# Both transposes of the global probabilities and the next pair's scores in one stop between the products

## The chip, the cores and the metric

The kernel runs on one core of a Trainium2 chip. The metric is the device time of one execution in microseconds (us), as the median of several executions; lower is better. TensorE (PE in the profile) does matrix products and transposes into PSUM banks, ScalarE (ACT), VectorE (DVE) and GpSimd (POOL) do the element-wise work, SyncE (SP) issues the transfers between HBM and SBUF. [...]

## The reference, cut to what matters

Eight batches, eight heads of size 64, 512 local and 32 global tokens. Attention comes first; its output, as rows of 512 channels over 32 + 512 tokens, goes through a feed-forward block ("channel mix") with a hidden width of 1024.

```python
# attention: a local token sees all 32 global keys and the local keys within 32 places
s_g = scale * q_g @ concat(k_g, k_l).T;  out_g = softmax(s_g) @ concat(v_g, v_l)
s_l = concat(scale * q_l @ k_g.T, where(|i - j| <= 32, scale * q_l @ k_l.T, -1e9))
out_l = softmax(s_l) @ concat(v_g, v_l)
x = concat(out_g, out_l) as (8, 544, 512)
# channel mix
xk = mu_k * x + (1 - mu_k) * x_prev;  xr = mu_r * x + (1 - mu_r) * x_prev
k  = relu(xk @ w_k) ** 2
out = sigmoid(xr @ w_r) * (k @ w_v)
```

Everything is float32. The large products of the channel mix are each made of three reduced-precision products of high and low parts (high by high, high by low, low by high), so every operand exists as a pair: xkh and xkl, xrh and xrl, bh and bl, wk_h and wk_l.

## The kernel before, in words

**The work in a step.** While the channel mix of one batch runs, the attention of the next batch is made in its gaps. `batch_of_heads()` yields attention in four-head halves ("pairs" of units, two pairs to a batch), and the channel mix is a generator that yields after each product of 24 matmuls of 128x256, about 2.7 us of TensorE. A string in the table BATCH (L1352) says in which order the two take turns: F is one product, A is one *stop*, the piece of attention that stands between two products. The order in which the code emits TensorE's instructions is the order in which TensorE runs them, since `in_line` (L149) chains each to the one before.

**The stops of a pair.** `attention()` (L917) yields these stops for a pair:
- T: transposes of the local probabilities Pt (L439, shown as ps_t or ps_s <- ident,Pt), copied to SBUF by ACT at L448;
- U0: `transposes_global(Pg, 0)`, three transposes of the global probabilities Pg into one PSUM bank, which two ACT copies (L532 and L538) take to the tensor PT;
- U1: `transposes_global(Pg, 1)`, three more, with one ACT copy (L532), and behind them in the same stop S, the scores of the next pair (ps_s <- raw_qk);
- GW: the next pair's global scores G, and W, the products of probabilities and values (ps_s <- PT,raw_v), after which the next raw_v are loaded.

The last pair of all has no next pair and so neither S nor G.

**Banks.** From the second batch on `psum(tag)` hands out banks by MIDDLE_USE (L132): "m" (products) has three, "s" (scores, W, some transposes) four, and "t" (transposes) has **one**. What takes bank t waits until the copy has read what was there before.

**What ACT, DVE and POOL do in between.** After the score stop the softmax pieces wait in the queue `softmaxes`; `soften()` emits one at each F. For each keys product ACT does relu (L694) and square (L695, to a block B). From the third batch on (FROM = 2) the second product of the block, k by w_v, uses seven products in place of eight, on sums and differences of blocks (B11, B12, ..., T1 to T4). `Keys.difference` makes such a T on DVE (L772); `Keys.part` makes its high part on ACT (L779, bh) and its low part bl (L780): on DVE where the block's name begins with B, on POOL where it begins with T. The other operand of these products, a, is loaded from scratch by SP (L338).

**The end.** `end()` runs the last products alone, with no attention in between; a table of steps gives what is prepared after each product, and `at("T3", 1)` stands first in it.

Of the kernel before, what the change touches and what calls it, by code (L numbers as in the profile page):

```python
# [10 lines left out]
F32 = mybir.dt.float32  # L11
# [9 lines left out]
P = 128  # L21
# [14 lines left out]
def window_of(i):  # L36
    return min(max(i - 1, 0), NW - 1)
# [28 lines left out]
FIRST = """  # L66
    @qk0 @qk1 B.1 B.0 G.a+5 g.a @qk3 S.a1 @qk2 F.a @ch5 R.a1.0 S.a0 E.a1.0 R.a1.1 @ch4 J.a R.a0.0 A.5 G.b
    R.a0.1 E.a1.1 S.b0 E.a0.1 g.b M.a I.a1 A.4 N.a1.1 f.S.b1+4 U.a.1 @ch2 @v0 D.5 U.a.0 @v1 E.a0.0 u.a.1 S.b1 I.a0 N.a1.0
    T.a1.0+2 u.a.0 D.4 N.a0.1 N.a0.0 @ch1 T.a1.1 C.a1.0 C.a1.1 F.b T.a0.1 T.a0.0 C.a0.1 A.2 R.b0.0 D.2 C.a0.0
    R.b0.1 @ch6 J.b A.1 E.b0.0 H.5 R.b1.0 D.1 H.2 @ch3 A.6 L.5 @qkc1 f.G.c+3 P.a0 p.a0 H.4 f.G.c+4 P.a1 E.b0.1 R.b1.1 I.b0 L.2  # L70
    @qkc0 p.a1 @ch0 @ch7 M.b X.0.k.0 N.b0.0 G.c T.b0.0 E.b1.1 Y.0.k.0 X.0.r.0 D.6 g.c C.b0.0 Z.0.k.0 E.b1.0 A.0
    A.3 U.b.1 u.b.1 N.b0.1 T.b0.1 A.7 D.3 C.b0.1 U.b.0 I.b1 u.b.0 D.7 Y.0.r.0 Z.0.r.0 S.c1 R.c1.0 H.6 L.4 @v2
    D.0 @v3 P.b0 H.1 H.7 @ch10 N.b1.0 p.b0 S.c0 N.b1.1 @qkd0 L.6 X.0.k.2 H.3 E.c1.0 T.b1.0 L.1 A.10 L.3 T.b1.1
    Y.0.k.2 H.0 R.c1.1 @ch11 C.b1.1 L.7 D.10 A.11 C.b1.0 X.0.r.2 L.0 E.c1.1 Z.0.k.2 R.c0.0 @ch9 @qkd1 D.11 I.c1
    H.10 F.c P.b1 L.10 K.0.0 p.b1 Y.0.r.2 H.11 R.c0.1 k.0.0 E.c0.1 A.9 N.c1.1 L.11 G.d T.c1.1 N.c1.0 Z.0.r.2 D.9
# [15 lines left out]
def local_global_attention_then_rwkv_ffn(  # L91
# [10 lines left out]
    nc = tc.nc  # L102
    B = qk.shape[0]
# [37 lines left out]
    def psum(tag):  # L141
        n = turn[tag] = turn.get(tag, -1) + 1
        pool = use[tag][n % len(use[tag])]
        return pool.tile([P, 512], F32, tag="ps", name=f"ps_{tag}")
# [17 lines left out]
    def transpose(*a, **kw):  # L162
        return in_line(nc.tensor.transpose(*a, **kw))  # L163
# [12 lines left out]
    for r in range(len(ROWS[0])):  # L176
        rows, same = slice(r * CK, (r + 1) * CK), {}
        for g, row in enumerate(ROWS):
            at = START[window_of(row[r])] // CK
# [3 lines left out]
        for (n, off), gs in same.items():  # L183
# [5 lines left out]
            part = edge[rows, (off + 1) // 2, rows]  # L189
# [93 lines left out]
    FROM = 2  # L283
# [65 lines left out]
    def load_qk(s, pool=rawp, tag=""):  # L349
        s.qk = pool.tile([P, K0 + SK + 2 * NC], F32, tag="qk" + tag, name="raw_qk")  # L350
        nc.sync.dma_start(out=s.qk, in_=qk[s.b, s.c])
        s.q, s.k, s.mu = s.qk[:, QG:K0], s.qk[:, K0:K0 + SK], s.qk[:, K0 + SK:]

    def load_v(s, pool=rawp, tag=""):
        raw = pool.tile([P, NV], F32, tag="v" + tag, name="raw_v")
        nc.sync.dma_start(out=raw, in_=v[s.b, s.c])
        s.v = raw.rearrange("p (h w d) -> p h w d", h=2, d=D)
# [68 lines left out]
    def scores(slots):  # L426
        r = Scores(slots)
        r.make()
        r.read(0)
        r.read(1)  # L430
        return r

    def whole(s):
        return [(s, p) for p in range(2)]
# [24 lines left out]
    class Global:  # L459
# [4 lines left out]
        whole = None  # L464
# [53 lines left out]
    def tails(rows, at, step, n):  # L518
        first = PT[rows, 0, 0, at:at + CK]
        return bass.AP(first.tensor, first.offset, (first.ap[0], (PART, 4), (step, n), (1, CK)))  # L520

    def transposes_global(Pg, part, n_fill=0):
        ts = ((0, 1, 5), (2, 3, 4))[part]
        tp = psum("t")[:, :3 * P].rearrange("p (t n) -> p t n", n=P)
        fill(tp[:, 0], n_fill)
        for n, t in enumerate(ts):
            lo, hi = (t * (W - CK), (t + 1) * (W - CK)) if t < 5 else (NGK - W, NGK)
            transpose(tp[:hi - lo, n], Pg[:, lo:hi], ident)

        def copy():  # L530
            n, rows = (2 if 5 in ts else 3), slice(0, W - CK)
            nc.scalar.copy(  # L532
                tails(rows, TAIL[ts[0]], TAIL[ts[1]] - TAIL[ts[0]], n),
                tp[rows, 0:n].rearrange("p t (u q) -> p u t q", u=4),
            )
            if 5 in ts:
                rows = slice(P - 2 * CK, P)
                nc.scalar.copy(tails(rows, TAIL[5], CK, 1), tp[rows, 2:3].rearrange("p t (u q) -> p u t q", u=4))  # L538
        return copy
# [73 lines left out]
    class Tokens:  # L613
# [19 lines left out]
        def part(self, x):  # L633
            return (self.xk_h, self.xk_l) if x == "k" else (self.xr_h, self.xr_l)
# [105 lines left out]
    class Keys:  # L740
# [30 lines left out]
                self.k[out] = self.k[place] if place else self.block(out)  # L771
            nc.vector.tensor_sub(self.k[out][i], self.k[a][i], self.k[b][i])  # L772

        def part(self, b, i):
            tags = Keys.PARTS[Keys.n_parts % len(Keys.PARTS)]
            Keys.n_parts += 1
            h, l = (self.tokens[0].two(mlp, f"b{x}", F32R, tag) for x, tag in zip("hl", tags))
            val = self.k[b][i]
            nc.scalar.copy(h, val)  # L779
            (nc.vector if b[0] == "B" else nc.gpsimd).tensor_sub(l, val, h.bitcast(F32))  # L780
            self.parts.setdefault(b, []).append((h, l))

        def made(self, b, i):
# [133 lines left out]
    def attention(pairs, R, Pg):  # L917

        for pair, nxt in zip(pairs, pairs[1:] + [None]):
            for s in nxt or ():  # L920
                load_qk(s)
            halves_of = [iter(range(2)) for _ in R]
            for j, r in enumerate(R):
                whole_unit = pair[0].b > FROM + 1
                for copies in [["t", "s"]] if whole_unit else [["t"], ["t"]]:
                    done = [transposes(r, next(halves_of[j]), j, bank=bank) for bank in copies]
                    for copy in done:
                        copy()
                    yield
            transposes_global(Pg, 0)()  # L930
            yield
            transposes_global(Pg, 1)()
            if nxt:
                R = [scores(whole(s)) for s in nxt]
                halves = list(product(R, range(2)))
                halves[0][0].exps(0)
                for (r, h), (r_next, h_next) in zip(halves, halves[1:]):
                    softmaxes.append((lambda r=r, h=h: r.norm(h), lambda r=r_next, h=h_next: r.exps(h)))
            yield
            if nxt:  # L940
                G = Global(nxt)
                G.make("s", "t")
                G.read()
                Pg = G.Pg
            weighted(pair, True)()
            if nxt:
                softmaxes.append((lambda: R[1].norm(1), G.exps))
                softmaxes.append((G.norm,))
            for s in nxt or ():
                load_v(s)  # L950
            yield pair[1].c + 1 == NC
# [47 lines left out]
    group_g = {y: Global(pair) for y, pair in pair_of.items()}  # L999
    first = tokens_of(0)  # L1000
    mus = {"k": mu_k_sb, "r": mu_r_sb}
    copies, banks, got = {}, {}, {}
# [4 lines left out]
    def fill(bank, n):  # L1007
        while n > 0:
            k = min(n, 4)
            blocks = bass.AP(ident.tensor, ident.offset, (ident.ap[0], (0, k), (1, P)))  # L1010
            matmul(bank[:, :k * P].rearrange("p (t n) -> p t n", t=k), ident, blocks, start=True, stop=True)
            n -= k
# [19 lines left out]
        group_g[y].make(*("tt" if y in "ab" else "st"), n_fill, (lambda: group["a1"].ahead(1)) if y == "a" else None)  # L1032

    def step_transposes_global(y, part, n_fill=0):
        copies["U", y, part] = transposes_global(group_g[y].Pg, int(part), n_fill)

    def step_weighted(x, n_fill=0):
        if len(x) > 1:
# [166 lines left out]
    with tc.manual_schedule(engines={mybir.EngineType.SP}):  # L1205
        for x in FIRST:
            x, _, n_fill = x.partition("+")
            kind, at = (x[0], x[1:]) if x[0] == "@" else (x[0], x[2:])
# [136 lines left out]
    def keys_at(b):  # L1345
# [4 lines left out]
    ends, held_writes = [], []  # L1350
    FILL_AT = {(B - 2, 1): (1, 0)}
    BATCH = {  # L1352
        FROM - 1: "AFAFAFAFAF" "AFFAFFF" "AFAFAFAFAF" "AFFAFFF",
        FROM: "AFAFAFAFAF" "AFAF" "AFAFAFAFAF" "AFFAFF",
        None: "AFFAFFAF" "AFFAFF" "AFFAFFAF" "AFFFAFF",
    }
    last = first[1]
    change_use(MIDDLE_USE)
    for b in range(1, B):
        if b < B - 1:  # L1360
# [4 lines left out]
            last = keys_at(b) if b >= FROM else batch.last  # L1365
    t, = final.tokens
# [3 lines left out]
    last = keys_of[B - 1]  # L1370

    def end():
        keys, gates = final.keys(t), t.gates()
        values, outs = chain(ends[0], last.values_2()), final.values_of_one()
        at = last.part
        todo = (
            lambda: (at("T3", 1), at("T1", 0), last.difference("T4", 1)),
            lambda: (at("T1", 1), at("T4", 0), held_writes.pop()()),
            lambda: t.mixing("r0"),
            lambda: (at("T4", 1), at("B22", 0)),  # L1380
            lambda: t.mixing("r2"),
            lambda: at("B22", 1),
            lambda: final.part("B11", 0),
            lambda: (final.part("B11", 1), final.part("B21", 0)),
            lambda: final.part("B21", 1),
        )
        for n, x in enumerate("VKVKVKVKVEGEGEE"):
            next({"K": keys, "V": values, "E": outs, "G": gates}[x], None)
            if n < len(todo):
                todo[n]()  # L1390
            yield
    for _ in end():
        pass
# [49 lines left out]
```

## Time and profile before

| | |
|---|---|
| median of 3 runs | 631.14 us (630.88 to 631.23) |
| the profiled execution | 631.95 us, of which the profile's span is 630.2 us |
| TensorE busy | 621.4 us, 99% of the span |
| DVE, ACT, POOL busy | 437.8 (69%), 381.8 (61%), 335.2 us (53%) |
| granted TensorE clock | tenths of full speed: 9 (90% or more) in all 40 slices |
| chain of waits | 82% TensorE, then DVE 5%, DMA 3%, POOL 3% |

The profile is one execution as the hardware profiler recorded it. In a row of the timeline the first number is the start in us from the beginning of the span, the second the time from the start of the first to the end of the last of the instructions that the row takes together. Matmuls overlap, so their pace is read from the distance between starts, not from the length of one.

### The profile page before, as it was taken

The page shows a single profiled execution, that of the slowest core. Times are in us where ns is not written, and L with a number is a line of the kernel's source. Part 1 is how long each engine was busy: PE and PEld are TensorE (multiplying, and loading weights), DVE is VectorE, ACT ScalarE, POOL GpSimd, SP SyncE. Part 2 cuts the span into 40 slices and gives each one's busy share as a digit, 9 for nine tenths or more (in the row PEclk, how much of TensorE's full clock was granted, in tenths as well). Part 3 has the DMA queues.
Part 4 walks back from the last instruction along what each step waited for, and adds up shares of the span by engine and source line. Part 5 has one row for each costly group of instructions (what it writes and reads, how often), then busy time and mean ns, then how long its engine had stood idle before and what let it go on. Part 6 is the DMA issues. An engine that isn't in the chain of part 4 may idle for free.

```text
span 630.2 us, 20466 instructions
## 1 busy us (share of the span) xinstructions
PE 621.4 (99%) x8354; PEld 592.7 (94%) x8354; DVE 437.8 (69%) x1238; ACT 381.8 (61%) x1154; POOL 335.2 (53%) x292
## 2 busy tenths in 40 slices
PE   7999999999999999999999999999999999999997
PEld 4789999999999999999999999999999999999997
DVE  8999983659888487666686677667686647446750
ACT  6999967264373778575747757575757744433531
POOL 4786555536855335845375535745375535533740
PEclk9999999999999999999999999999999999999999
DMA  8965561457393546275563928275553734467673
GB/s 335 407 206 207 206 230 63 167 206 263 105 304 128 200 164 228 66 272 210 173 245 122 355 92 340 83 266 201 190 228 118 286 102 136 129 222 238 202 244 138
DMA packets 43278, 127.29 MB, mean 202 GB/s; under 512 B 3760, under 2 KB 20656, under 8 KB 43184
## 3 DMA queue, kind: packets, MB, share of 16 engines
q1 hardware_dynamic: 43184, 125.98, 56.1%
q8 instruction: 66, 1.08, 0.6%
q14 instruction: 28, 0.23, 0.1%
HBM read 108.66 MB, written 17.30 MB: 200 GB/s over the span
## 4 chain that ended last, share of the span: by engine, by line
PE 82%; DVE 5%; DMA 3%; POOL 3%; issue 1%; ACT 1%; SPq 0%; DVEq 0%; POOLq 0%
PE ps_m L160 64%; PE ps_s L160 12%; PE ps_t L163 3%; DMA w<-w_v 1%; PE ps_s L163 1%; DMA raw_qk<-qk 1%; DMA raw_v<-v 1%; DVE a L299 1%; POOL wk_l L271 1%; DVE diff L656 1%; POOL Pt L420 1%; POOL w L252 1%; PE ps_t L160 1%; DVE diff L651 0%; POOL wv_l L271 0%
## 5 line engine op out<-in xcount | busy, mean ns | idle before, releaser
L160 PE MATMUL ps_m<-xkh,wk_h 128*128 128x256 f32 x544 | 154.5, 284 | 0.0
L160 PE MATMUL ps_m<-xkh,wk_l 128*128 128x256 f32 x544 | 151.0, 278 | 0.0
L160 PE MATMUL ps_m<-xkl,wk_h 128*128 128x256 f32 x544 | 150.9, 277 | 0.0
L160 PE MATMUL ps_m<-bh,a 128*128 128x256 f32 x736 | 132.5, 279 | 0.0
L160 PEld LDWEIGHTS ps_m<-bh,a 128*128 128x128 f32 x736 | 113.5, 188 | 0.0
L420 POOL TENSOR_TENSOR Pt<-Pt,ssum 128x512 f32<-128x512 f32 x64 | 69.4, 1089 | 81.7 <-ACT Pt L409 38.4
L409 ACT ACTIVATE Pt<-Pt,m 128x128 f32<-128x128 f32 x256 | 99.5, 397 | 11.9 <-DVE m L402 11.8
L160 PEld LDWEIGHTS ps_m<-xkh,wk_h 128*128 128x128 f32 x544 | 102.4, 188 | 3.7 <-issue 1.2
L160 PEld LDWEIGHTS ps_m<-xkh,wk_l 128*128 128x128 f32 x544 | 102.3, 188 | 0.0
L160 PEld LDWEIGHTS ps_m<-xkl,wk_h 128*128 128x128 f32 x544 | 102.3, 188 | 0.0
L160 PE MATMUL ps_m<-bl,a 128*128 128x256 f32 x368 | 102.1, 277 | 0.0
L694 ACT ACTIVATE relu<-ps_m 128x512 f32<-128x512 f32 x52 | 31.0, 596 | 76.6 <-PE ps_m L160 76.6
L160 PE MATMUL ps_m<-xrh,wr_h 128*128 128x256 f32 x272 | 76.8, 282 | 0.0
L661 POOL TENSOR_TENSOR xkl<-xfull,xkh 128x512 fp32r<-128x512 f32 x30 | 40.2, 1340 | 66.1 <-DVE ssum L361 42.8
L160 PE MATMUL ps_m<-xrl,wr_h 128*128 128x256 f32 x272 | 75.3, 277 | 0.0
L160 PE MATMUL ps_m<-xrh,wr_l 128*128 128x256 f32 x272 | 75.3, 277 | 0.0
L402 DVE CUSTOM_DVE_ANT_0 Pt<-ps_s,masks 128x128 f32<-128x128 f32 x256 | 55.8, 284 | 22.3 <-PE ps_s L160 22.3
L160 PEld LDWEIGHTS ps_m<-bl,a 128*128 128x128 f32 x368 | 69.2, 188 | 0.0
L661 POOL TENSOR_TENSOR xrl<-diff,xrh 128x512 fp32r<-128x512 f32 x30 | 41.1, 1368 | 41.3 <-DVE xrh L660 26.1
L780 DVE TENSOR_TENSOR bl<-B,bh 128x512 fp32r<-128x512 f32 x40 | 37.8, 960 | 30.0 <-ACT bh L779 29.7
L780 POOL TENSOR_TENSOR bl<-B,bh 128x512 fp32r<-128x512 f32 x36 | 49.0, 1382 | 17.5 <-ACT bh L779 11.7
L656 DVE SCALAR_TENSOR_TENSOR diff<-diff,mu_r_sb,xT 128x256 f32<-128x256 f32 x56 | 57.0, 1057 | 0.0
(158 smaller groups left out, 1474.4 us busy)
## 6 DMA issues: line engine op xcount, KB each, us to landing
a<-scratch SPq DMA_DIRECT2D x92, 512.0 KB, 4.7
raw_v<-v SPq DMA_DIRECT2D x32, 896.0 KB, 8.4
raw_qk<-qk SPq DMA_DIRECT2D x32, 628.0 KB, 4.9
out_l<-gate SPq DMA_DIRECT2D x32, 256.0 KB, 2.2
w<-w_k SPq DMA_DIRECT2D x8, 512.0 KB, 11.9
w<-w_v SPq DMA_DIRECT2D x8, 512.0 KB, 3.6
w<-w_r SPq DMA_DIRECT2D x4, 512.0 KB, 3.8
scratch<-wv_h SPq DMA_DIRECT2D x8, 256.0 KB, 2.3
```

Of the source, the lines that this page charges most:

```text
L160: return in_line(nc.tensor.matmul(*a, **kw))
L163: return in_line(nc.tensor.transpose(*a, **kw))
L252: nc.gpsimd.tensor_scalar(word(n, F32, 1), word(n, F32, 1), REBIAS, 1.0, op0=ALU.mult, op1=ALU.mult)
L271: nc.gpsimd.tensor_sub(part_of_weights(n, "l"), word(n, F32, 0), part_of_weights(n, "h").bitcast(F32))
L299: nc.vector.tensor_sub(s.bitcast(F32R), s, hs.bitcast(F32))
L402: nc.vector.tensor_tensor_reduce(out=self.Pt[:, i], in0=self.place(t, n, h), in1=masks[:, 2 * self.slots[t][1] + n], op0=ALU.add, op1=ALU. ...
L409: nc.scalar.activation(self.Pt[:, i], self.Pt[:, i], AF.Exp, bias=self.low_x[:, i:i + 1], scale=-1.0, accum_out=self.ssum[:, i:i + 1],)
L420: nc.gpsimd.tensor_mul(self.Pt[:, some], self.Pt[:, some], inv.unsqueeze(2).to_broadcast([P, 4, W]))
L656: nc.vector.scalar_tensor_tensor(self.shape(xf[:, j]), self.shape(d[:, j]), mu[:, c0 + j:c0 + j + 1], self.prev(c0 + j), op0=ALU.mult, op1 ...
L661: nc.gpsimd.tensor_sub(lo[:, both], xf, hi[:, both].bitcast(F32))
L694: nc.scalar.activation(rk, kp, AF.Relu)
L780: (nc.vector if b[0] == "B" else nc.gpsimd).tensor_sub(l, val, h.bitcast(F32))
```

## The change

`transposes_global` gets the bank as a parameter. `attention()` no longer yields between U0 and U1, and puts the scores between them: the stop is now U0, S, U1. U0 stays in bank t, except for the last pair, where it takes a bank of "s". A pair has one stop fewer, so the strings in BATCH lose one A per pair; the number of F's stays the same. With batch 3 and later, a first pair had T FF T FF U0 F (U1 S) FF (GW) FF and now has T FF T FF (U0 S U1) FFF (GW) FF; a second pair had T FF T FF U0 F (U1 S) FFF (GW) FF and now has T FF T FF (U0 S U1) FFF (GW) FFF, so that its GW comes one product earlier. In batches 1 and 2 the joint stop stands where U1 stood. `Keys.part` gets a parameter `by`, the engine of its subtraction, and `at("T3", 1)` in `end()` passes VectorE.

```diff
-    def transposes_global(Pg, part, n_fill=0):
+    def transposes_global(Pg, part, bank="t", n_fill=0):
         ts = ((0, 1, 5), (2, 3, 4))[part]
-        tp = psum("t")[:, :3 * P].rearrange("p (t n) -> p t n", n=P)
+        tp = psum(bank)[:, :3 * P].rearrange("p (t n) -> p t n", n=P)
...
-        def part(self, b, i):
+        def part(self, b, i, by=None):
...
             nc.scalar.copy(h, val)
-            (nc.vector if b[0] == "B" else nc.gpsimd).tensor_sub(l, val, h.bitcast(F32))
+            (by or (nc.vector if b[0] == "B" else nc.gpsimd)).tensor_sub(l, val, h.bitcast(F32))
...
-            transposes_global(Pg, 0)()
-            yield
+            transposes_global(Pg, 0, "t" if nxt else "s")()
+            R = [scores(whole(s)) for s in nxt or ()]
             transposes_global(Pg, 1)()
             if nxt:
-                R = [scores(whole(s)) for s in nxt]
                 halves = list(product(R, range(2)))
...
     BATCH = {
-        FROM - 1: "AFAFAFAFAF" "AFFAFFF" "AFAFAFAFAF" "AFFAFFF",
-        FROM: "AFAFAFAFAF" "AFAF" "AFAFAFAFAF" "AFFAFF",
-        None: "AFFAFFAF" "AFFAFF" "AFFAFFAF" "AFFFAFF",
+        FROM - 1: "AFAFAFAFF" "AFFAFFF" "AFAFAFAFF" "AFFAFFF",
+        FROM: "AFAFAFAFF" "AFAF" "AFAFAFAFF" "AFFAFF",
+        None: "AFFAFF" "AFFFAFF" "AFFAFF" "AFFFAFFF",
     }
...
-            lambda: (at("T3", 1), at("T1", 0), last.difference("T4", 1)),
+            lambda: (at("T3", 1, nc.vector), at("T1", 0), last.difference("T4", 1)),
```

TensorE's queue at the first pair of batch 4 in the kernel before: ps_m rows are matmuls of a keys product (24 in each), ps_t <- ident,Pg are U0 (2 + 1) and U1 (3), ps_s <- raw_qk the scores S (each of which the trace shows as two).

```order
L160 MATMUL ps_m<-xkh,wk_l 128x256
L163 MATMUL ps_t<-ident,Pg 96x128 x2
L163 MATMUL ps_t<-ident,Pg 128x128
L160 MATMUL ps_m<-xkh,wk_h 128x256
...
L160 MATMUL ps_m<-xkh,wk_l 128x256
L163 MATMUL ps_t<-ident,Pg 96x128 x3
L160 MATMUL ps_s<-raw_qk 32x128 x64
L160 MATMUL ps_m<-xkh,wk_h 128x256
```

The same place in the changed kernel:

```order
L160 MATMUL ps_m<-xkl,wk_h 128x256
L160 MATMUL ps_m<-xkh,wk_l 128x256
L163 MATMUL ps_t<-ident,Pg 96x128 x2
L163 MATMUL ps_t<-ident,Pg 128x128
L160 MATMUL ps_s<-raw_qk 32x128 x64
L163 MATMUL ps_t<-ident,Pg 96x128 x3
L160 MATMUL ps_m<-xkh,wk_h 128x256
```

The product between U0 and U1 has gone behind the stop, and S, not a product, now lies between the two groups that share bank t.

ACT's queue there, in the kernel before: relu and B belong to the keys product that ended just ahead of U0, bh to another block, 96x4x2x32 and 64x4x32 are the copies of U0, 96x4x96 is the copy of U1.

```order
L694 ACTIVATE relu<-ps_m 128x512
L695 ACTIVATE B_5632<-relu 128x512
L779 CAST bh<-B_4458 128x512
L532 COPY PT<-ps_t 96x4x2x32
L538 COPY PT<-ps_t 64x4x32
L694 ACTIVATE relu<-ps_m 128x512
L695 ACTIVATE B_5632<-relu 128x512
L779 CAST bh<-B_4459 128x512
L532 COPY PT<-ps_t 96x4x96
```

And in the changed kernel:

```order
L694 ACTIVATE relu<-ps_m 128x512
L695 ACTIVATE B_5632<-relu 128x512
L779 CAST bh<-B_4458 128x512
L532 COPY PT<-ps_t 96x4x2x32
L538 COPY PT<-ps_t 64x4x32
L532 COPY PT<-ps_t 96x4x96
L409 ACTIVATE Pt,ssum<-Pt,m 128x128 x4
L694 ACTIVATE relu<-ps_m 128x512
```

The copies of U0 still stand behind relu, B and bh; the copy of U1 has moved ahead of the next relu.

DVE's queue in `end()`, as the difference of the two kernels (bl <- B_9230 is the low part of T3's second half, which lies in B_9230):

```order
 L772 TENSOR_TENSOR B_8990<-B_8990,T_9474 128x512
 L858 TENSOR_TENSOR sum<-ps_m,sum 128x512
+L780 TENSOR_TENSOR bl<-B_9230,bh 128x512
 L772 TENSOR_TENSOR B_8990<-B_8990,T_9474 128x512
 L867 TENSOR_TENSOR sum<-ps_m,sum 128x512
```

The subtraction is new between L858 and the second L772; POOL's queue loses the same row, which stood behind bl <- B_9229.

## Rows read from the trace of the kernel before

**Rows 1.** The profile's page, its fourth part: the chain that ended last, share of the span by engine.

```profile
PE 82%; DVE 5%; DMA 3%; POOL 3%; issue 1%; ACT 1%; SPq 0%; DVEq 0%; POOLq 0%
```

**Rows 2.** Timeline of TensorE at the first pair of batch 4: U0, the product behind it, U1, S, the next product. Columns: start, time, engine, line, operation, out <- in, tile of the array, shape, count.

```profile
330.72 0.49 PE L163 MATMUL ps_t<-ident,Pg 128*96 128x128 f32 x3
330.97 0.37 PE L160 MATMUL ps_m<-xkh,wk_h 128*128 128x256 f32 x1
331.17 0.28 PE L160 MATMUL ps_m<-xkl,wk_h 128*128 128x256 f32 x1
...
333.67 0.28 PE L160 MATMUL ps_m<-xkh,wk_l 128*128 128x256 f32 x1
333.79 0.49 PE L163 MATMUL ps_t<-ident,Pg 128*96 128x128 f32 x3
334.21 2.05 PE L160 MATMUL ps_s<-raw_qk 64*32 64x128 f32 x128
336.19 0.38 PE L160 MATMUL ps_m<-xkh,wk_h 128*128 128x256 f32 x1
336.41 0.28 PE L160 MATMUL ps_m<-xkl,wk_h 128*128 128x256 f32 x1
```

**Rows 3.** Timeline of TensorE in batch 0, where scores are followed by a product (52.03) and, at another place, by transposes (59.53).

```profile
52.03 1.16 PE L160 MATMUL ps_s<-raw_qk 64*32 64x128 f32 x64
53.11 0.39 PE L160 MATMUL ps_m<-xkh,wk_h 128*128 128x256 f32 x1
...
59.53 1.16 PE L160 MATMUL ps_s<-raw_qk 64*32 64x128 f32 x64
60.62 1.09 PE L163 MATMUL ps_t<-ident,Pt 128*128 128x128 f32 x8
61.46 0.36 PE L160 MATMUL ps_m<-xrh,wr_h 128*128 128x256 f32 x1
```

**Rows 4.** Timeline of ACT at the stop of rows 2.

```profile
330.98 0.60 ACT L694 ACTIVATE relu<-ps_m 128x512 f32<-128x512 f32 x1 [3.84 <-PE ps_m L160]
...
332.20 0.60 ACT L779 CAST bh<-B 128x512 fp32r<-128x512 f32 x1
332.71 0.36 ACT L532 COPY PT<-ps_t 96x256 f32<-96x256 f32 x1
333.08 0.26 ACT L538 COPY PT<-ps_t 64x128 f32<-64x128 f32 x1
```

**Rows 5.** Timelines of ACT and of TensorE where a transpose waits for ACT's copy of its bank (batch 2).

```profile
215.66 0.56 ACT L448 COPY PT<-ps_t 128x512 f32<-128x512 f32 x1
...
216.37 0.63 PE L163 MATMUL ps_t<-ident,Pt 128*128 128x128 f32 x4 [0.25 <-ACT PT L448]
```

**Rows 6.** Pieces of the chain that ended last, all on TensorE: start, time, output, line, count of matmuls. The first is a product behind transposes that had waited, the other three are products behind scores, in batches 1, 3 and 6.

```profile
217.00 2.74 PE ps_m L160 x24
...
127.91 5.85 PE ps_m L160 x48
...
265.77 5.66 PE ps_m L160 x48
...
477.55 5.85 PE ps_m L160 x48
```

**Rows 7.** Timelines near the end: TensorE's weight loads, its matmuls, and POOL's row that covers them.

```profile
591.40 0.19 PEld L160 LDWEIGHTS ps_m<-bl,a 128*128 128x128 f32 x1
...
591.45 0.33 PE L160 MATMUL ps_m<-bl,a 128*128 128x256 f32 x1
591.62 0.40 PE L160 MATMUL ps_m<-bh,a 128*128 128x256 f32 x2
...
588.02 7.27 POOL L780 TENSOR_TENSOR bl<-B,bh 128x512 fp32r<-128x512 f32 x5 [1.28 <-ACT bh L779]
```

**Rows 8.** Busy time of TensorE in two stretches of 30 us, ahead of rows 7 and behind them: stretch, length, busy us (matmuls), granted clock, share of the DMA engines, GB/s.

```profile
560.00:590.00 30.00, 30.00 (x267) 1.00 0.71 226
593.00:623.00 30.00, 30.00 (x257) 1.00 0.70 225
```

**Rows 9.** Timeline of DVE ahead of rows 7 and behind them.

```profile
589.01 1.18 DVE L772 TENSOR_TENSOR B<-B,T 128x512 f32<-128x512 f32 x1
593.00 0.69 DVE L867 TENSOR_TENSOR sum<-ps_m,sum 128x512 f32<-128x512 f32 x1 [2.81 <-PE ps_m L160]
```

**Rows 10.** Timelines of DVE, POOL and TensorE around the second half of T2 in batch 4 (bl <- T).

```profile
310.78 0.69 DVE L772 TENSOR_TENSOR T<-B,B 128x512 f32<-128x512 f32 x1 [3.09 <-ACT B L695]
...
314.01 0.72 DVE L495 CUSTOM_DVE_ANT_0 Pg<-ps_s,nothing,mg 128x480 f32<-128x480 f32 x1
...
321.16 1.59 POOL L661 TENSOR_TENSOR xrl<-diff,xrh 128x512 fp32r<-128x512 f32 x1 [0.98 <-DVE xrh L660]
323.85 1.44 POOL L780 TENSOR_TENSOR bl<-T,bh 128x512 fp32r<-128x512 f32 x1
...
325.18 0.37 PE L160 MATMUL ps_m<-bh,a 128*128 128x256 f32 x1
```

**Rows 11.** The piece of the chain that holds most of the GW stop ahead of rows 10 (four transposes stand in front of it).

```profile
308.30 4.27 PE ps_s L160 x116
```

**Rows 12.** Timelines of POOL and TensorE: the same subtraction at the start of the last batch, and the first matmul that needs it.

```profile
531.52 1.30 POOL L780 TENSOR_TENSOR bl<-T,bh 128x512 fp32r<-128x512 f32 x1 [1.83 <-ACT bh L779]
...
534.33 0.28 PE L160 MATMUL ps_m<-bl,a 128*128 128x256 f32 x1
```

More of the change, by code (lines that the diff above doesn't have):

```diff
@@ L1034, in step_transposes_global @@
     def step_transposes_global(y, part, n_fill=0):
-        copies["U", y, part] = transposes_global(group_g[y].Pg, int(part), n_fill)
+        copies["U", y, part] = transposes_global(group_g[y].Pg, int(part), n_fill=n_fill)
     def step_weighted(x, n_fill=0):
```

## Prediction

> **What bounds the kernel now.** I read the chain of waits first: 82% of it is TensorE [rows 1], so what counts is how TensorE's own row of instructions is paced and where it stops; DVE, ACT and POOL matter only where TensorE comes to wait for them. Second came TensorE's timeline around one pair's stops, which gives the price of each passage between kinds of work [rows 2, 3]. Third, ACT's timeline there, because bank t is freed by ACT [rows 4, 5]. Fourth, the chain's pieces of 48 product matmuls: behind scores the same 48 take 5.66 us in one place and 5.85 in others [rows 6], so products seem to have two paces. Fifth, the end: behind one late weight load TensorE goes over to the slower pace and keeps it to the end: 257 matmuls in 30 us against 267 ahead of it, 116.7 ns each against 112.4, the granted clock 1.00 in both [rows 7, 8].
>
> **The change part by part.** *Fewer passages.* A product behind a product costs 0.114 us per matmul (2.74 / 24) [rows 6]. Before: from U0's first transpose to the second matmul behind it 0.45 us (330.72 to 331.17), with 0.12 to get into the transposes (333.67 to 333.79), less two pitches of 0.114, is 0.34; the U1 and S stop, 333.67 to 336.41, less the same two, is 2.51 [rows 2]. Together 2.85 per pair. After: 0.12 into U0, 0.42 from U0 to the first score (333.79 to 334.21), 1.98 for the scores (334.21 to 336.19) [rows 2], then transposes straight behind scores. That passage is in the trace: 64 scores to the first transpose take 1.09 us (59.53 to 60.62) and to a product 1.08 (52.03 to 53.11), so it costs no more, and eight transposes to the product take 0.84 [rows 3], of which five pitches of 0.11 (0.25 for three, 330.72 to 330.97) are to be taken off: 0.29. With 0.20 to the second matmul and less two pitches the stop is 2.78. The starts are rounded to 0.01, so of the 0.07 I take 0.06; bounds 0 and 0.11 (if the first transpose behind scores cost no more than one behind a product). There are twelve pairs; the last has no scores, and the second of batch 1 stands ahead of a stretch in which the chain leaves TensorE for DVE, so I count ten: -0.6 us.
>
> The rule that speaks against this is the Trainium skill's, in "TensorEngine Tiling (Array Packing)", section "Tiling Modes": a change of tiling mode drains TensorE. The scores are 64x32 tiles, the rest is not, and both kernels go into that mode and out of it once per pair; by the rule alone the first part would be nothing and the sum -0.3 us. The 1.09 and 1.08 us agree that leaving the mode has one price whatever follows; the rest, the transposes' own entry and exit, is what the rows give back.
>
> *Bank t.* U1 must wait until ACT has copied U0 out of the one bank t. Before, a whole product lay between them; now only the scores do: 0.42 + 1.98 = 2.40 us from U0's start to U1. At batch 4's first pair ACT has relu, the square and a cast bh ahead of the copies, starts the relu at 330.98 and ends the second copy at 333.34, 2.62 us behind U0's start (330.72) [rows 2, 4]. A transpose that waited for such a copy began 0.15 us behind the copy's end (216.22 to 216.37) [rows 5]. So U1 comes at 2.77, a wait of 0.37, of which about 0.03 comes back because the first transpose's passage lies in it: 0.34. The order shows the same three instructions ahead of the copies in the first pairs of batches 3 to 6 and in the second of batch 2, hence five: +1.7 us. In the other pairs no cast stands there, and the copies end before the scores do. Bounds 0.2 to 0.45 each (ACT's relu may start a little earlier or later against U0), 1.0 to 2.3 together.
>
> *Pace behind the stop.* The product behind the stop now follows transposes, not scores. Behind transposes that had waited, 24 matmuls took 2.74 us, the faster pace [rows 6]. Three pieces of 5.85 (the first at 127.91, the last at 477.55) would come down to 5.66: 3 x 0.19 = -0.6 us. Bounds 0, if something else sets the pace, and -0.9, if the stops between them gain half of that too.
>
> *The end.* The late load at 591.40 is that of a low part bl, made on POOL, which works through five such subtractions from 588.02 on, 1.45 us each; the second, that of T3, ends at about 591.0 [rows 7]. On DVE it stands ahead of the L772 of 589.01; a subtraction of the same size there takes at most 1.18, so it ends by 590.2, over a microsecond before 591.4, and what it delays has 2.81 us of idle time behind it [rows 9]. POOL's later ones come 1.45 us earlier. Then TensorE keeps the faster pace from 591.6 to about 627: 35.3 x (1 - 257 / 267) = 1.3 us, and the late load's 0.06: -1.4 us. Bounds 0 (something else is late next, or the pace drops anyway) and -1.4.
>
> *GW one product earlier in second pairs.* The keys product that stood ahead of GW now comes behind it and ends about 4.5 us later (4.27 and four transposes) [rows 11]. From it comes the difference T2 (DVE, 310.78), whose successors on DVE and POOL end with bl at 325.29 [rows 10]. Before, the square stood behind other work on ACT; if it now follows at once, T2 comes at about 313.9. DVE's reads of the global scores (0.72 the longer one) leave the way, as GW comes earlier, so of the 10.4 us from T2 to xrl about 9.4 are left: xrl at 323.3, bl done at 323.3 + 1.59 + 1.44 = 326.3. It is needed by the thirteenth matmul of a product that starts at 325.18, 325.18 + 0.2 + 11 x 0.114 = 326.6. So 1.3 us of reserve become 0.3. I cost it at nothing; without that cover each of batches 4 to 6 pays 0.3 to 0.7. Softmax pieces, raw_qk and raw_v come earlier, which only helps; loads of a that wait for the moved product come about 3 us later and have, as an estimate from the same times, a microsecond or more in hand.
>
> **Sum.** -0.6 + 1.7 - 0.6 - 1.4 = -0.9 us on the profiled execution's 631.95 (span 630.2 and 1.75 around it), which is 0.81 above the median of the runs; on the median 631.14 - 0.9 = 630.2 us.
>
> **The rivals.**
> 1. *U1 does not wait*, because ACT gets to its copies about 0.4 us sooner than at batch 4. For it: everything on ACT follows TensorE, and the wait is small beside 2.6 us of ACT work. Against: the three instructions ahead are there by the order, and their times are steady. -0.9 - 1.7 = -2.6: 628.5.
> 2. *Slower: POOL's T2 at the last batch.* There bl runs 531.52 to 532.82 and is needed at 534.33 [rows 12]; by the working above the moved product takes 1.0 of these 1.5 us. If bl comes late, its load sets the slower pace as at 591.4, and no stop stands between there and the end to set it back: 93 us of products, some 800 x 4.3 ns = 3.4 us, of which the kernel before pays the last 1.3 too, so 2.1 more, and the end's gain is gone. -0.9 + 1.4 + 2.1 = +2.6: 633.7. It decides from 0.5 us beyond what I reckon. For it: this is the one place where the change makes a subtraction later in front of a long run of products. Against: the reserve.
> 3. *The passages give nothing*, because the way into the scores' tiles and out of them costs the same wherever it stands, or the pace behind the stop does not change: -0.9 + 0.6 = -0.3, so 630.8. For it: 1.09 against 1.08 us [rows 3]. Against: the product behind transposes at its faster pace [rows 6].
> 4. *The change doesn't do at the end what it says*: the next low part is late as well, or the slower pace comes without it. -0.9 + 1.4 = +0.5, so 631.6.
>
> **How the numbers follow.** The forecast has 0.55, its own range 629.5 to 630.8 (the wait's bounds). Rival 1 has 0.12, rival 2 0.10, rival 3 0.13, rival 4 0.10. 0.2% is 1.26 us, about what a measurement of this kernel can tell from no change: faster is under 629.9, slower over 632.4. Faster: rival 1 and a third of the forecast, 0.30. Slower: rival 2, 0.10. Same: the rest, 0.60. The range 628.8 to 632.3 leaves out rival 2 and the lower half of rival 1; it takes in POOL's T2 late in batches 4 to 6 (up to +2.1).
>
> **What would show it.** Passages: at batch 4's first pair, from the last product matmul to the second behind the stop, 3.0 us plus the wait. Bank t: U1's transposes with idle time ahead of them put down to ACT's L538, 0.3 to 0.4 us, in five stops and not in the others. Pace: the 72 products behind a stop (three F) at 8.2 us. The end: no late load at 591, and 267 matmuls in the last 30 us. T2: bl <- T done before the middle of its product in batches 4 to 7. Wrong it would be if U1's wait stood in all eleven stops, or if a new late load appeared in front of a long run of products.

## The result and the profile after

The changed kernel takes 637.52 us (median of 4 runs, 635.15 to 641.0) against 631.18 (630.88 to 632.25) before: ratio 1.009, 95% interval 1.0065 to 1.0114. It is slower, outside the predicted range and on the other side of no change. The profiled execution took 635.15 us, 3.2 more than that of before.

From the page of the changed kernel, its head and the first line of its fourth part (the chain that ended last, share of the span by engine):

```profile
span 633.4 us, 20434 instructions
...
PE 77%; DVE 5%; POOL 4%; DMA 3%; ACT 3%; issue 1%; POOLq 0%; SPq 0%; ACTq 0%; DVEq 0%
```

TensorE's share of the chain has gone from 82% [rows 1] to 77%; POOL and ACT have more of it. The waits of TensorE's weight loads from 120 us on name what is new (us in total, times, longest):

```profile
PEld ps_t L163 <- ACT PT L538: 2.3, 5, 0.5
PEld ps_m L160 <- POOL bl L780: 2.1, 4, 0.8
```

Five waits for the copy of U0 and four for a low part of POOL; neither line is there in the kernel before.

**The joint stop.** TensorE's timeline at the first pair of batch 4, and three of ACT's rows there (relu, the square, the second copy of U0), to be held against [rows 2, 4]:

```profile
332.34 0.28 PE L160 MATMUL ps_m<-xkh,wk_l 128*128 128x256 f32 x1
332.46 0.49 PE L163 MATMUL ps_t<-ident,Pg 128*96 128x128 f32 x3
332.88 2.06 PE L160 MATMUL ps_s<-raw_qk 64*32 64x128 f32 x128
335.13 0.53 PE L163 MATMUL ps_t<-ident,Pg 128*96 128x128 f32 x3 [0.19 <-ACT PT L538]
335.42 0.37 PE L160 MATMUL ps_m<-xkh,wk_h 128*128 128x256 f32 x1
335.62 0.28 PE L160 MATMUL ps_m<-xkl,wk_h 128*128 128x256 f32 x1
```

```profile
332.72 0.60 ACT L694 ACTIVATE relu<-ps_m 128x512 f32<-128x512 f32 x1 [4.37 <-PE ps_m L160]
333.40 0.64 ACT L695 ACTIVATE B<-relu 128x512 f32<-128x512 f32 x1
...
334.81 0.26 ACT L538 COPY PT<-ps_t 64x128 f32<-64x128 f32 x1
```

U1 starts 2.67 us behind U0 (335.13 - 332.46); the scores would have let it go at 2.40. From the last product matmul to the second behind the stop it is 3.28 us, where 3.0 plus the wait was forecast: the wait is 0.27.

**The late low part.** Pieces of the chain in batch 4 (the places of [rows 10, 11]), and the subtraction's counterpart in the last batch [rows 12]; start, time, what:

```profile
310.75 2.95 PE ps_m L160 x24
...
315.01 0.69 DVE T L772
...
324.46 0.44 DVE xrh L660
...
325.06 1.56 POOL xrl L661
326.62 1.70 POOL bl L780
...
328.37 4.27 PE ps_m L160 x35
...
537.03 1.72 POOL bl L780
...
538.79 91.30 PE ps_m L160 x803
```

The keys product that GW was moved past ends at 313.70, T2's difference follows it, and then everything that stands behind T2 on DVE and POOL; TensorE stops in the middle of a product until bl is there, at 328.37. The same chain holds in batches 5 and 7, a shorter one in 6.

**The end.** Matmuls in two stretches of 30 us, the counterpart of [rows 8]:

```profile
560.00:590.00 30.00, 30.00 (x267) 1.00 0.71 231
593.00:623.00 30.00, 30.00 (x267) 1.00 0.76 248
```

The late load at 591 and the slower pace behind it are gone.

**The sum of the profiled executions.** Worked out from TensorE's starts from 121 us (the 501st product matmul) to the last one, 505.6 us before and 509.0 after. A distance between two product matmuls counts against 0.1134 us; stops are taken from the last matmul ahead to the first behind, and the passages take in the first distance behind the stop, too.

| term | forecast | measured |
|---|---|---|
| passages into and out of the stops of U0, U1, S | -0.6 | -0.7 |
| GW stops (52.7 to 52.2 us in eleven) | none | -0.5 |
| waits for bank t (joint stops 32.2 us, 30.9 in e4, which has none) | +1.7 | +1.3 |
| waits for bl inside products | 0 | +2.1 |
| slower pace between the stops | -0.6 | +2.4 |
| slower pace at the end | -1.4 | -1.3 |
| sum | -0.9 | +3.3 |

### The profile page after: what moved, and what is told of

Its sections match the earlier page's. It is cut to its first block, busy times and chain, and to the rows that moved or that the text cites. A ratio compares the mean times of both kernels' runs of the same rounds, so it can differ in the third digit from the quotient of the medians.

```text
span 633.4 us, 20434 instructions
## 1 busy us (share of the span) xinstructions
PE 622.8 (98%) x8354; PEld 593.0 (94%) x8354; DVE 448.8 (71%) x1239; ACT 382.4 (60%) x1154; POOL 335.1 (53%) x291
## 4 chain that ended last, share of the span: by engine, by line
PE 77%; DVE 5%; POOL 4%; DMA 3%; ACT 3%; issue 1%; POOLq 0%; SPq 0%; ACTq 0%; DVEq 0%
PE ps_m L160 62%; PE ps_s L160 11%; PE ps_t L163 3%; DMA w<-w_v 1%; POOL bl L780 1%; DVE diff L656 1%; POOL xrl L661 1%; ACT B L695 1%; DMA raw_qk<-qk 1%; DMA raw_v<-v 1%; DVE xfull L656 1%; PE ps_s L163 1%; ACT relu L694 1%; DVE diff L651 1%; POOL wk_l L271 1%
## 5 line engine op out<-in xcount | busy, mean ns | idle before, releaser
L160 PEld LDWEIGHTS ps_s<-PT,raw_v 128*64 128x64 f32 x1568 | 49.9, 138 | 7.0 <-issue 5.2
```

What stands on the lines that cost most here:

```text
L160: return in_line(nc.tensor.matmul(*a, **kw))
```

## The experiments

Times are held against runs of the kernel before that were taken beside them, with medians of 632.1 to 632.8 us; kernels that were not measured beside each other are compared by their ratios to it. "Slower share" is counted in TensorE's timeline from 120 to 535 us, some 2500 product matmuls: those that start more than 115.6 ns (midway between the two paces) behind the one before, without the first behind a stop and without waits. Two theories were there at the start: A, the late T2, and B, the wait for bank t. A third, C, came out of the first four experiments.

| kernel | stop ends in | slower share | waits for bl | us, median | ratio to before (95%) |
|---|---|---|---|---|---|
| before | S | 18% | none | 631.18 | 1 |
| changed | U1 | 41% | 4 | 637.52 | 1.0090 (1.0065 to 1.0114) |
| e1 GW back | U1 | 51% | none | 634.95 | 1.0041 (1.0024 to 1.0057) |
| e2 only GW early | S | 21% | 4 | 639.61 | 1.0128 (1.0094 to 1.0161) |
| e3 only the end | S | 18% | none | 631.54 | 0.9983 (0.9968 to 0.9999) |
| e4 U1 in m | U1 | 44% | 4 | 636.39 | 1.0066 (1.0045 to 1.0087) |
| e5 GW back, U1 in m | U1 | 53% | none | 634.84 | 1.0037 (1.0017 to 1.0056) |
| e6 mixing first | U1 | 43% | none | 632.48 | 1.0000 (0.9978 to 1.0021) |
| e7 before, S U1 | U1 | 36% | none | 633.00 | 1.0002 (0.9980 to 1.0024) |
| e8 U0 U1 S, U1 in m | S | 21% | 4 | 635.08 | 1.0053 (1.0025 to 1.0081) |
| e9 e8, mixing first | S | 22% | none | 631.29 | 0.9994 (0.9979 to 1.0008) |
| e10 e4, mixing first | U1 | 66% | none | 635.13 | 1.0046 (1.0030 to 1.0062) |
| e11 e2, mixing first | S | 11% | none | 631.26 | 0.9991 (0.9976 to 1.0006) |
| e12 changed, again | U1 | 48% | 4 | 637.99 | 1.0088 (1.0057 to 1.0119) |

**e1: GW back in its place.**

```diff
-        None: "AFFAFF" "AFFFAFF" "AFFAFF" "AFFFAFFF",
+        None: "AFFAFF" "AFFFAFF" "AFFAFF" "AFFFFAFF",
```

> The change with one edit: in second pairs of batch 3 and later the GW stop goes back behind a fourth product (T FF T FF U0SU1 FFFF GW FF), as late as in the kernel before. Theory A (GW one product earlier puts the keys product behind GW, T2's difference comes late on DVE, and bl <- T, last on POOL, comes late for TensorE in batches 4 to 7): no wait for POOL's bl there, 631 to 632.2 us, executions within 1 us of each other. Theory B (U1's wait for bank t and what it does to the pace is the loss): no better than the changed kernel, 635 to 638, and scattered as it is.

634.95 us, +0.41%. The waits for bl are gone, executions lie within 3 us (634.0 to 636.8), and the time is some 3 us under that of the changed kernel, so A is a part. It is not all: 2.6 us stay, where at most 1 us was expected. B stays too, with the same row of five waits and 2.3 us.

**e2: nothing but GW early, on the kernel before.**

```diff
-        None: "AFFAFFAF" "AFFAFF" "AFFAFFAF" "AFFFAFF",
+        None: "AFFAFFAF" "AFFAFF" "AFFAFFAF" "AFFAFFF",
```

> The kernel before with nothing but the GW stop of second pairs one product earlier (T FF T FF U0 F U1S FF GW FFF); stops and engines as before. Theory A: slower by 3 us or more, 634 to 639, with TensorE waiting for bl <- T in batches 4 to 7 and executions several us apart. Theory B: no difference, 631.2.

639.61 us, +1.28%. Its waits of weight loads:

```profile
PEld ps_m L160 <- POOL bl L780: 5.8, 4, 1.9
```

The moved GW alone costs more than the whole change; the joint stop is not needed for it. A holds, with a time just over its range.

**e3: nothing but the end, on the kernel before.**

```diff
-            lambda: (at("T3", 1), at("T1", 0), last.difference("T4", 1)),
+            lambda: (at("T3", 1, nc.vector), at("T1", 0), last.difference("T4", 1)),
```

> The kernel before with only T3's second subtraction in end() on VectorE. If the late load at 591 is what sets the slower pace: 267 matmuls in 30 us to the end and 629.9 us (-1.3). If the pace there does not come from it: 631.2, no difference.

631.54 against 632.64 us, -0.17% (0.9968 to 0.9999). The last stretch:

```profile
593.00:623.00 30.00, 30.00 (x267) 1.00 0.70 229
```

The pace is as forecast, 267 in place of 257; the gain in time is small, and its interval ends just under 1. That the late load alone brings the slower pace is not shown: the traces of e2 and e11, which lack this edit, have the same break in the stream there (in e11 the matmul behind the one with bl at 591.15 comes 0.17 us later, as in the kernel before) and kept the faster pace. The same stretch in e11:

```profile
593.00:623.00 30.00, 30.00 (x267) 1.00 0.69 225
```

With the slower pace behind this load are the kernel before, e7 and e16 (257, 258, 258). So the edit takes away a break that was followed by the slower pace in three traces of five.

**e4: U1 in a bank of m, on the changed kernel.**

```diff
-            transposes_global(Pg, 1)()
+            transposes_global(Pg, 1, "m" if nxt else "t")()
```

> The change with U1 in a bank of m, so that it waits for no copy of ACT. Theory A: the five waits for ACT's L538 go (1.5 to 2 us), the waits for bl stay: 633 to 636, still scattered. Theory B: 630 to 631, no scatter.

636.39 us, +0.66%. No wait for ACT's L538 is left, the eleven joint stops take 30.9 us in place of 32.2, and the waits for bl are as they were (2.6 us in 4). In the traces B is worth 1.3 us and cannot be the whole loss. Two things were not as A had it: the time lies just over its range, and the four executions lie within 1 us, not scattered.

What A and B leave was then looked for in the pace. In both kernels with the old stops about a fifth of the products went at the slower one, in the three with the joint stop over two fifths, also behind GW and behind the transposes T, where nothing was changed. That is theory C.

**e5: both waits taken away.** The edits of e1 and e4 together.

> The change with GW of second pairs back in its place and U1 in a bank of m: neither POOL's bl nor the copy in bank t is waited for. If these two waits (theories A and B) are the whole loss, the fewer passages (about -1.2 us) and the end (-1.2) are left: 2 us faster than before. Theory C (a stop that ends in transposes leaves TensorE in the slower product pace more often, in the products behind it and behind the stops that follow; products from 120 to 535 us at the slower pace: 14 to 20% in the kernels with the old stops, 40% and more with the joint one, each 4.3 ns): the 25% more of 2500 products, 2.7 us, eat it up: before +0 to +1.5.

634.84 us, +0.37% or 2.3 us, with no wait for bl or for L538. So A and B are not the whole; slower share 53%. That is as C said, and it costs somewhat more than it forecast. Against e1, which has the wait for bank t, nothing is gained (1.0037 and 1.0041), though the wait is gone.

**e6: the mixing ahead of T2.**

```diff
-                16: lambda: (this.difference("T2", 1), mix_next("k0")),
+                16: lambda: (mix_next("k0"), this.difference("T2", 1)),
```

> The change with one line of the step table turned round: behind the keys product of step 16, the next batch's mixing k0 is issued ahead of T2's second difference, so that DVE does not wait for the product before it mixes. Theory A: GW may stay early, no wait for POOL's bl in batches 4 to 7, 2 us and more below the changed kernel, before +1.5 to +3, and little scatter. If the lateness came from elsewhere (POOL's own queue): waits for bl as in the changed kernel.

632.48 us, level with the kernel before and some 5.5 under the changed one. DVE and POOL at the place of the late low part:

```profile
312.05 0.87 DVE L656 SCALAR_TENSOR_TENSOR xfull<-diff,mu_k_sb,xT 128x256 f32<-128x256 f32 x2
...
314.96 1.01 DVE L772 TENSOR_TENSOR T<-B,B 128x512 f32<-128x512 f32 x1 [0.98 <-ACT B L695]
...
321.62 0.43 DVE L660 CAST xrh<-diff 128x512 fp32r<-128x512 f32 x1
...
323.90 1.60 POOL L780 TENSOR_TENSOR bl<-T,bh 128x512 fp32r<-128x512 f32 x1
```

T2 comes at 314.96, no earlier than in the changed kernel (315.01), but bl starts at 323.90 in place of 326.62 (in the changed kernel's chain): what was late was not T2 but the mixing that stood behind it in DVE's queue, and POOL's xrl that waits for the mixing and stands ahead of bl. This place of the cause is shown. The gain is greater than the forecast of 2 us and more, and greater than the waits for bl that the traces of the changed kernel show (2.1 to 2.6 us); how the rest comes about is not shown. e6 still has the five waits for L538 and a slower share of 43%.

**e7: the scores ahead of U1, in the old stop of the kernel before.**

```diff
-            transposes_global(Pg, 1)()
-            if nxt:
-                R = [scores(whole(s)) for s in nxt]
+            R = [scores(whole(s)) for s in nxt or ()]
+            transposes_global(Pg, 1)()
+            if nxt:
```

> The kernel before with U1 behind the scores in its old stop (U0 F S U1), nothing else: a product now follows transposes instead of scores in eleven places. The prediction's pace term: 0.6 us faster. Theory C: slower by 1.5 to 3 us, with over 30% of the products from 120 to 535 us at the slower pace. If the pace has nothing to do with the order in the stop: no difference.

633.00 against 632.51 us, ratio 1.0002 (0.9980 to 1.0024): neither the 0.6 us of gain nor the loss that C named. In the profiled execution the slower share is 36%, twice that of before, as C said; the stops themselves are about 0.6 us cheaper there. The interval holds both a gain of 1.3 us and a loss of 1.5, so by its time this one is inconclusive.

**e8: the scores last in the joint stop.**

```diff
-            R = [scores(whole(s)) for s in nxt or ()]
-            transposes_global(Pg, 1)()
+            transposes_global(Pg, 1, "m" if nxt else "t")()
+            R = [scores(whole(s)) for s in nxt or ()]
```

> The change with U1 in a bank of m and ahead of the scores: one stop U0 U1 S that ends with scores, as the old one did. Theory C: 15 to 25% of the products from 120 to 535 us at the slower pace, 2 us below e4 (joint stop in the same banks, transposes last), before +1 to +2.5, the waits for bl being left. If the order in the stop does not matter: as e4, before +4.

635.08 us, +0.53%; slower share 21% against 44% in e4. The share is as C said. The time is not: it lies 2.6 us over the kernel before by the medians and 3.4 by the ratio, more than the +1 to +2.5 expected, and e8 is not shown to be faster than e4 (1.0053 and 1.0066, the intervals overlap). Its executions lie from 633.2 to 639.8 us.

**e9 and e10: without either wait, the scores last or in the middle.** e8 and e4, each with e6's line.

> e8 (joint stop U0 U1 S, U1 in a bank of m, scores last) with the step-16 line of e6 turned round: no wait for bl, no wait for bank t, the faster pace mostly kept, the end on VectorE. If A, B and C are all of the loss: e8's trace less its 3.0 us of stalls, 1.5 us below the kernel before, 0.2 to 0.3% faster, about as e3. If something else is lost in the joint stop: no faster than the kernel before.

> The same two mends with the scores in the middle, as the change has them (U0 S U1, U1 in m, step 16 turned round). It differs from e9 only in the place of the scores. Theory C: 40 to 50% of the products from 120 to 535 us at the slower pace against 20% in e9, 2 us slower than e9, about as the kernel before. If the place of the scores does not matter: as e9.

631.29 and 635.13 us, 0.9994 (0.9979 to 1.0008) and 1.0046 (1.0030 to 1.0062): 3.8 us between two kernels that differ in the place of eleven blocks of scores alone. The order alone is not the whole of it, though: e6 and e10 differ in U1's bank alone, both have the transposes last, and e10, which waits for no copy, is the slower one (1.0046 against 1.0000, the intervals apart); e6 is level with e9. What the bank does here is open: e1 and e5 differ in it too and take the same time, and e4 is not slower than the changed kernel. The trace of e10, with its 66%, is that of the slowest of its nine executions. Pieces of the chain behind the stop of batch 5's first pair, first e9, then e10:

```profile
405.76 8.37 PE ps_m L160 x72
...
418.66 5.66 PE ps_m L160 x48
...
425.19 5.46 PE ps_m L160 x48
...
431.52 5.46 PE ps_m L160 x48
```

```profile
409.61 8.48 PE ps_m L160 x72
...
422.63 5.85 PE ps_m L160 x48
...
429.35 5.66 PE ps_m L160 x48
...
435.88 5.66 PE ps_m L160 x48
```

The first piece is the one behind the stop, the second stands behind GW, the others behind the transposes T. Behind the same kind of stop 48 products take 5.66 or 5.85, 5.46 or 5.66: in e10 the pace that the first piece got into (70 of its 71 distances are slower ones, in e9 2) comes back behind the next stops.

The traces of all eighteen runs show how. In TensorE's starts a run of products between two stops is nearly always at one pace throughout: of the 396 runs counted here, 389 have over 90% of their distances on one side of 115.6 ns. Each trace has eleven GW stops, with a run of products ahead of each and one behind it:

| run ahead of GW stands behind | runs | at the slower pace | run behind GW slower too |
|---|---|---|---|
| scores (seven traces) | 77 | 27 | 0 of 27 |
| transposes U1 (eleven traces) | 121 | 77 | 55 of 77 |

Where the run ahead of GW was at the faster pace (50 and 44 runs), the one behind it was never slower. So the slower pace comes more often behind transposes than behind scores, and only there does it outlast the GW stop.

e9 gains nothing beyond e3's end, though its passages are fewer, and 1.5 us were forecast: its traced execution has 2.3 us of slower pace against 1.9 in e3's, and one short wait of 0.2 us for L538.

**e11: e2 with the mixing first.** The edits of e2 and e6.

> e2 (the kernel before with GW of second pairs one product earlier) with step 16 turned round. Theory A in its exact form (T2's difference stands first in DVE's queue and holds up the mixing behind it while it waits for the later product): e2's 6 us of waits for bl are gone, the time is that of the kernel before within 1 us. If the moved GW costs in another way: still 3 us or more slower.

631.26 against 632.11 us (0.9976 to 1.0006), no wait for bl: with the order of the two lines turned, the early GW costs nothing. Theory A is shown in its exact form: between e2 and e11, which differ in the order of these two lines alone, lie some 8.6 us by the ratios.

**e12 to e15: the changed kernel again; e16: e2 again.**

> The changed kernel as it is, on the chip of these runs: 4 to 6 us above the kernel before, four waits for bl, about 40% of the products from 120 to 535 us at the slower pace; single executions 3 to 4 us apart, as the long run of products behind the last late bl falls into one pace or the other.

> The changed kernel, one more profiled execution. Its executions lie in two groups, 635 to 636.5 and 639 to 641 us, and all traces so far are of the lower one, with the 803 products behind the last late bl at the faster pace. If the upper group is that run of products at the slower pace (800 x 4.3 ns = 3.4 us): an execution of 638.5 us or more has about 257 matmuls in 560 to 590 us, one of 636.5 or less 267. If the scatter lies elsewhere (transfers at the start, the pace between the stops): 267 in both.

> As e13, another execution of the same kernel: 257 matmuls in 560 to 590 us if it takes 638.5 us or more, 267 if it takes 636.5 or less.

> As e13, a third execution of the same kernel: 257 matmuls in 560 to 590 us if it takes 638.5 us or more, 267 if it takes 636.5 or less.

> e2 once more (638.3, 638.4, 640.8 and 643.8 us so far; the trace was of one of the lower ones). The same question: an execution of 641 us or more with 257 matmuls in 560 to 590 us, one of 639 or less with 267, if the long run of products behind the late bl makes the groups.

e12: 637.99 us, +5.9, the loss of the first measurement again. e13, e14 and e15 took 637.16, 637.51 and 637.36 us, all between the two groups. The stretch from 560 to 590 us, first e13, then e14:

```profile
560.00:590.00 30.00, 30.00 (x257) 1.00 0.70 217
```

```profile
560.00:590.00 30.00, 30.00 (x267) 1.00 0.71 221
```

So the long run behind the last late bl does fall into one pace or the other, in the same kernel and behind the same wait. But e13 had only 23% of the earlier products at the slower pace, e14 and e15 49 and 45%, which makes most of the difference good; the rest is in the time up to the 501st product matmul, 120.8, 121.7 and 122.2 us in e13, e14 and e15. e16 (639.78 us) has 268, and 258 from 593 on, where the first trace of e2 has 267. The two groups of the expectation are not there as such: an execution's time is the sum of several such falls and of what differs at the start. Of the nine traces with a late bl at the start of the last batch, e13 alone has the slower pace behind it. No execution above 639.8 us was traced, so that both together make 641 is an inference.

## Why the prediction was wrong, point by point

- **Fewer passages, -0.6:** right, -0.7. Transposes straight behind scores cost what batch 0 had shown [rows 3]. The Trainium skill ("TensorEngine Tiling (Array Packing)", section "Tiling Modes") says that a change of tiling mode drains TensorE, and gives no price; by that rule alone nothing would have come of it. The 0.7 us do not contradict it: the ways into the scores' tiles and out of them stay as many, and the transposes' own are fewer. A gain that the prediction had not is the 0.5 us of the GW stops; no run explains it.
- **Bank t, +1.7:** right in place and number (five stops), a little large: 1.3 us in the traces (0.27 at batch 4's first pair, not 0.37). In the measured times no gain came of taking it away: e5 against e1 none, e10 against e6 a loss.
- **Pace behind the stop, -0.6: this step failed, by 3 us.** It took one run behind waited-for transposes, 24 matmuls at the faster pace [rows 6], for a rule: behind transposes fast, behind scores slow. The runs show the opposite tendency. The sign that the prediction named, 72 products in 8.2 us, stands in the changed kernel's chain behind the stop of batch 4's first pair (8.18) and not behind the one ahead of it (8.48, at 297.73). In the ten traces of a joint stop that ends in transposes the slower share is 23 to 66%, in nine of them over 40, and 36% in e7; in the seven traces of a stop that ends in scores it is 11 to 22%. Nor does it stay with the run behind the stop, as the step had it: behind transposes it outlasts the unchanged GW stop in 55 of 77 cases, behind scores in none of 27. What this costs in time is shown less well than the share: e9 against e10 3.8 us, e7 against the kernel before and e8 against e4 no difference clear of the noise. Why the way out of the stop decides over later pieces is open.
- **The end, -1.4:** right in the traced execution, -1.3; alone, e3 gained 0.17%. But the late load is not always followed by the slower pace (e2 and e11 kept the faster one), so that the trace of before showed its full price was in part luck.
- **GW one product earlier, costed at nothing: this step failed, by 2.1 us of waits in the traced execution; undone by e6, it gives back the whole loss against the kernel before (1.0090 to 1.0000).** The chain was named rightly and T2 came when it was reckoned to (315.01, less 0.9 us by which everything was late by then). But from T2 to the end of bl 13.3 us passed where 12.4 had been reckoned. The mixing came late: xrl started 10.05 us behind T2, not 9.4, and bl took 1.70 us, not 1.44. DVE's reads of the global scores did leave the way, as reckoned, but one row of DVE took up what they left:

```profile
317.91 2.69 DVE L651 TENSOR_TENSOR diff<-xT 128x256 f32<-128x256 f32 x2
```

  These two subtractions had taken 1.73 us in the kernel before. POOL works beside this row (xkl and Pt, 317.84 to 320.31), while the like row at 315.62, with POOL idle, took 0.76; that the one makes the other longer is a reading of these rows, which no run tests. A reserve of 0.3 us out of a long sum of durations was no reserve, and the upper end of the price that the prediction gave for its loss (0.7 us a batch) was met in batches 4 and 5 (0.7 and 0.8 us; 0.3 in 6 and in 7).
- **Rival 2** had the right place and the right side, at a chance of 0.10. It came true in the last batch as a late bl; its price, the whole of the last run at the slower pace, is what e13 shows, and the other eight traces with that late bl do not.
- **Rival 1** (no wait at bank t), **3** and **4** did not happen.

The median lies further off than the traced execution because that one was the fastest of the four.

## What to carry to other kernels

Where a step is moved past another, look first for a difference or copy that waits for the moved step at the head of another engine's queue: what it delays is everything behind it, and turning two lines round (e6, e11) can be worth more than the move. A reserve that is a small remainder of a long sum should be priced as if it were gone. And where the last fifth of a microsecond per stop is at issue on a full TensorE, count the pace of the products behind the stops as well as the stops: here the slower share hung on whether scores or transposes came last, and in one pair of three (e9, e10) 3.8 us went with it.

## What the runs showed of the hardware that was not expected

At a granted clock of 1.00 in both stretches of [rows 8], and of 0.999 or 1.000 as the mean of each traced execution, products of 128x256 run at 113.4 or at 117.8 ns from start to start; a pace once taken mostly lasts until the next stop or wait, at most 803 matmuls here, and can come back behind it (55 of 77 GW stops). A late weight load is followed by the slower pace in one execution and by the faster in another (e13 and e14, same kernel, behind waits of the same length). Single executions differ by 5 us and more (the kernel before: 630.3 to 635.4 us beside the experiments); the two paces are part of that, and the time up to the 501st product matmul another (120.8 to 122.2 us in the five traces of the changed kernel). One trace of each kernel compares two draws as well as two kernels; the shares over many traces are what separates the two forms of the stop.
